# Turning SA and v as one 128-column operand, longer load rows, 320 early slots and a new order of steps in a fused attention and expert kernel

## The chip, the cores and the metric

The kernel runs on one core of one Trainium2 chip. A core has five engines with one instruction stream each: PE (TensorE: matrix products and, beside them, weight loads), DVE (VectorE), ACT (ScalarE), POOL (GpSimd) and SP (SyncE, which here issues most transfers). Each executes its own instructions in order; they wait for each other by semaphores. The metric is the device time of one launch in microseconds, the median of three runs. For the kernel before it is 639.63 us (639.16 to 650.6).

## The reference

The inputs `r, k, v, w, a, b` have 4 batches, 8 heads, 768 steps and 40 columns. Each of the 32 (batch, head) pairs runs a recurrence over a 40 x 40 state; the outputs of all heads then form 3,072 rows of 320 columns that go through a top-1 mixture of 8 experts.

```python
for t in range(S):
    y[t] = r[t] @ state
    Sa = state @ a[t]
    state = state * w[t] - outer(Sa, b[t]) + outer(v[t], k[t])
x = y, as 3072 rows of 320
logits = x @ w_gate; e = argmax(logits); g = softmax(logits)[e]
slot of a row = its rank among the rows of expert e (kept if under 768)
out = g * (relu(x @ w1[e]) @ w2[e])
```

## The kernel before

**How the recurrence is tiled.** The 768 steps are NI = 6 blocks of 128, and each block has two chunks of 64 steps (C = 64, NQ = 12 chunks in all). A pair (`pr`) is two batches with all their heads, so there are two pairs and 2 x 12 = 24 units. Within a chunk the recurrence is written as matrix products and a triangular inverse; from chunk to chunk the state is handed on. R = 104 rows hold two batches of 40 columns, at rows 0 to 39 and 64 to 103.

**The steps of a block** (`prep`, L459). `load_w`, `load_a`, `load_kb` and `load_rv` bring the inputs in. `decay` runs two scans over w on VectorE (`scan_g` L484, `scan_p` L494) and multiplies a by one of them (`mul_a` L503); `decay_k` multiplies kb by the other (`mul_kb` L506, two products, c = 0 and 1). In `load_w` each of 128 rows is cut into 8 heads of 512 bytes, because the tile `px` has one column more per head, which a memset (L489) clears.

**The steps of a unit** (`unit`, L520, and `chain`, L773). `load_v` brings v as `vu` with time on the rows; `load_x` (`load_vT`, L532) brings the same v a second time, turned on the host, as half 0 of the tile `vT`. `kk` and `nn` are products of a and kb, `iden` turns kb (L574). Then `zz` and `sa` compute SA, which `take_sa` writes into `vu` beside v. `uT` (L824) turns SA alone, as 8 transposes with 64 rows and 64 columns (L829), and `take_uT` (L838) copies the result into half 1 of `vT`. `turn` and `take_turn` turn the state. `out` is `mT` (L875: for each of 16 (k, x, r) two products with 64 x 64 weights, one on v and one on SA), `take_m`, `yy` (outputs and new state), `take_snew` and `take_y`.

**The steps between units.** For each block there is a joint inverse over both pairs (`begin2` L731, then `inverse`, `join`, `lower`, `comb`; the group `comb_b` at L713 is one of 64 products), and, behind it, the gate: `turn_y` (L958, 8 transposes of 104 columns), `logits`, and `store_x`, which writes the rows to memory for the experts. Most matrix products go through the helper `mm`, whose one line is L403. Routing (`route`, L1241) runs once for each of the six blocks: `first` (the arg-max and its running counts), `count` (three products, L1258 on), `place`, `gates`, `hot_p`, `hot_j`, `tabled`, `fold`, and for the last two blocks `index`, which makes the row lists.

**The experts** (`expert`, L1480). The rows of an expert are gathered from memory by an indirect transfer (L1384), turned, multiplied with w1 (`p` steps, L1538), clipped (`h` steps, on ACT and VectorE), multiplied with w2 (`p` steps, L1407, in chunks of 128 rows with a last one of 64 where the count asks for it), scaled and scattered to the output by an indirect transfer (`o` steps, L1413). Each expert's weights are split into a high and a low half-width part, so a hidden or output block is a sum of several products. Experts 0 and 1 are done in two parts: EA = 384 slots whose rows were routed in the first five blocks, and EB = 128 late slots. The other six take MAIN = 448 slots at once.

**What sets the order.** `ORDER` (L29) is a list written out in full, one word per step, that covers scan, gate, routing and experts. `name*n` is the next n steps of that name, `name/m` takes the m-th of its alternatives (which engines do the copy), and `name~n` puts n filler products ahead of the step: `warm` (L192) issues them as 128 x 512 products of the identity into a buffer that the step is about to overwrite. `listed` (L199) turns the list into instructions; every engine then gets its own in just that order. The `needs`, `take` and `free` of a step (see the diff) name what it waits for and which buffers it draws and gives back. All transfers of `prep` and `unit` are issued by SP, in list order.

## Time and profile before

| | |
|---|---|
| median of 3 runs | 639.63 us (639.16 to 650.6) |
| the profiled execution | 641.26 us, of which its span 639.5 us |
| mean granted clock of PE | 0.899 of full speed |
| PE, matrix products | busy 589.2 us (92% of the span), 12,503 instructions |
| PEld, weight loads | busy 445.4 us (70%), 12,503 instructions |
| DVE | busy 424.1 us (66%), 958 instructions |
| ACT | busy 271.1 us (42%), 562 instructions |
| POOL | busy 102.7 us (16%), 146 instructions |

The span runs from the first to the last instruction of one profiled execution. Busy time is the time in which an engine had an instruction in flight, so the shares of different engines overlap. A weight load runs beside the product of the instruction before it. A granted clock of 1.0 is 2.4 GHz, 0.5 is 1.2 GHz.

### The profile page before, as it was taken

To read this page: it belongs to the slowest core of one execution; us is meant where nothing else is said; L and a number is where in the kernel's file an instruction comes from. 1 tells how busy PE (TensorE), PEld (TensorE's weight loads), DVE (VectorE), ACT (ScalarE), POOL (GpSimd) and SP (SyncE) were. 2 spreads that over 40 slices of the span, in tenths; PEclk is the share of its full clock that TensorE was granted. 3 is DMA by queue.
4 is the path that set the end of the run, shared out by engine and by line. 5 is a ranking of instruction groups with operands and counts; after the bars stand their busy time and mean duration, and the time that the engine had idled before them with its cause. 6 is when DMAs were issued, how large, how long until landed. Compare 5 with 4: busy or idle time off the path is not lost.

```text
span 639.5 us, 27724 instructions
## 1 busy us (share of the span) xinstructions
PE 589.2 (92%) x12503; PEld 445.4 (70%) x12503; DVE 424.1 (66%) x958; ACT 271.1 (42%) x562; POOL 102.7 (16%) x146
## 2 busy tenths in 40 slices
PE   1869999899999989998999999899999999989995
PEld 1559788788878878877878887666665555556653
DVE  7998897779779866987388675668235371644330
ACT  9324534433255342525263354534234553545221
POOL 6100000000010010000000000221512261542212
PEclk9765997989779986998599996899989999999999
DMA  6923047404327265143303143697659777676201
GB/s 186 215 70 101 5 114 170 115 21 138 112 64 202 62 130 153 39 131 82 121 25 112 37 144 98 167 192 210 168 128 247 213 201 171 195 198 176 60 21 37
DMA packets 78948, 80.43 MB, mean 126 GB/s; under 512 B 31731, under 2 KB 67669, under 8 KB 77860
## 3 DMA queue, kind: packets, MB, share of 16 engines
q1 hardware_dynamic: 75428, 68.92, 41.0%
q0 software_dynamic: 3392, 9.64, 5.2%
q8 instruction: 100, 1.64, 1.1%
q14 instruction: 28, 0.23, 0.1%
HBM read 63.39 MB, written 10.26 MB: 115 GB/s over the span
## 4 chain that ended last, share of the span: by engine, by line
PE 61%; issue 21%; POOL 6%; DMA 1%; ACT 1%; POOLq 1%; DVE 0%; SPq 0%; another core or an unknown queue 0%; ACTq 0%
PE pp L403 24%; PE p L403 18%; PE pp L1538 3%; POOL out_dram L1413 3%; PE pp L196 3%; PE p L196 3%; POOL a L1384 2%; PE pp L574 2%; PE pp L961 2%; PE p L866 2%; PE p L1407 2%; PE pp L829 2%; PE p L1065 1%; DMA xT<-a 1%; DMA vu<-in_moe_w_dram 1%
## 5 line engine op out<-in xcount | busy, mean ns | idle before, releaser
L1413 POOL DMA_INDIRECT out_dram<-tm,ri x32 | 35.1, 1096 | 114.6 <-ACT tm L1573 90.4
L403 PE MATMUL pp<-vu,bk 128*40 128x104 f32 (+1 forms) x768 | 43.2, 272 | 0.0
L457 DVE TENSOR_TENSOR vu<-pp,mask 128x1024 f32<-128x1024 f32 x24 | 29.3, 1220 | 17.8 <-PE pp L403 13.5
L403 PEld LDWEIGHTS pp<-vu,bk 128*40 128x40 f32 x768 | 37.3, 128 | 4.6 <-issue 3.3
L453 POOL TENSOR_SCALAR_AFFINE_SELECT tm<-tm 64x512 f32<-64x512 f32 x14 | 12.4, 887 | 162.1 <-ACT tm L450 161.6
L403 PE MATMUL p<-yq,ns 64*64 64x32 f32 x768 | 31.5, 244 | 7.0 <-ACT yq L157 4.2
L403 PE MATMUL pp<-rv,vT 64*64 64x64 f32 x1536 | 34.1, 242 | 3.3 <-issue 3.1
L153 POOL COPY x<-x 128x128 f16<-128x128 f16 x18 | 8.5, 476 | 173.4 <-ACT x L153 132.8
L403 PEld LDWEIGHTS p<-yq,ns 64*64 64x64 f32 x768 | 30.0, 164 | 8.5 <-issue 7.8
L403 PEld LDWEIGHTS pp<-rv,vT 64*64 64x64 f32 x1536 | 30.2, 154 | 7.6 <-issue 6.8
L403 PE MATMUL pp<-a,kb 64*64 64x64 f32 x768 | 19.7, 251 | 16.6 <-DVE px L489 13.9
L1538 PE MATMUL pp<-xT,ns 128*128 128x448 f16 (+2 forms) x192 | 34.2, 313 | 0.0
L1384 POOL DMA_INDIRECT a<-xd,ri x25 | 28.3, 1134 | 36.3 <-DVE gs L1302 26.6
L153 ACT COPY vu<-pp 64x320 f32<-64x320 f32 x42 | 17.6, 420 | 35.6 <-PE pp L403 30.7
L582 ACT ACTIVATE bk<-pp,sgn 128x320 f32<-128x320 f32 x48 | 22.6, 526 | 20.7 <-PE pp L574 15.6
L403 PE MATMUL p<-a,kb 64*64 64x64 f32 x768 | 31.2, 236 | 0.0
L403 PEld LDWEIGHTS pp<-a,kb 64*64 64x64 f32 x768 | 16.4, 159 | 20.9 <-issue 17.6
L1538 PE MATMUL pp<-xT,px 128*128 128x448 f16 (+2 forms) x128 | 29.3, 313 | 1.9 <-DVE nt L1546 1.9
L403 PEld LDWEIGHTS p<-a,kb 64*64 64x64 f32 x768 | 28.0, 149 | 4.1 <-issue 3.7
L490 DVE TENSOR_TENSOR_SCAN gx<-px,z 104x1032 f32<-104x1032 f32 x12 | 27.7, 2308 | 3.1 <-DMA px<-in_w_dram 2.8
L510 DVE TENSOR_TENSOR kb<-kb,gx 104x1024 f32<-104x1024 f32 x24 | 29.8, 1281 | 0.0
L1546 DVE SCALAR_TENSOR_TENSOR px<-pp,rv 128x448 f16<-128x448 f32 (+1 forms) x32 | 18.6, 602 | 16.5 <-ACT rv L1543 15.0
(246 smaller groups left out, 1458.3 us busy)
## 6 DMA issues: line engine op xcount, KB each, us to landing
vu<-in_moe_w_dram SPq DMA_DIRECT2D x32, 320.0 KB
kb<-in_kb_dram SPq DMA_DIRECT2D x24, 320.0 KB
px<-in_moe_w_dram SPq DMA_DIRECT2D x13, 512.0 KB
px<-in_w_dram SPq DMA_DIRECT2D x12, 512.0 KB
vu<-in_vt_dram SPq DMA_DIRECT2D x48, 128.0 KB
vT<-in_vx_dram SPq DMA_DIRECT2D x24, 256.0 KB
xd<-x SPq DMA_DIRECT2D x24, 192.0 KB
a<-in_a_dram SPq DMA_DIRECT2D x24, 160.0 KB
```

The source lines that it names most:

```text
L153: (e.copy if e is self.nc.scalar else e.tensor_copy)(out, in_)
L196: self.nc.tensor.matmul(x, self.spare[:, 0:P], self.spare[:, None, :].to_broadcast([P, 2, 2 * P]), start=True, stop=True, skip_group_check ...
L403: TT.matmul(out, l, r, start=start, stop=True, skip_group_check=True)
L457: V.tensor_mul(out, in_, m.to_broadcast(sh))
L490: V.tensor_tensor_scan(T["gx"][0:R, 0:H * (P + 1)][:, ::-1], T["px"][0:R].rearrange("p h t -> p (h t)")[:, ::-1], z2[0:R].rearrange("p h t ...
L510: V.tensor_mul(x, x, g[:, :, None, half(c)].to_broadcast([R, H, 2, C]))
L574: TT.transpose(p[:, x, h * D:h * D + D], T["kb"][half(x, D), h, c].rearrange("p z t -> p (z t)"), ident[half(x, D), C * x:C * x + D])
L582: A.activation(U["bk"][:, x].rearrange("p h d -> p (h d)"), U["pi"][:, x, 0:HD], AF.Copy, scale=sgn[:, x:x + 1])
L1384: nc.gpsimd.indirect_dma_start(out=xt(j)[:c].rearrange("p a c -> p (a c)"), out_offset=None, in_=src[:, :], in_offset=bass.IndirectOffsetO ...
L1413: nc.gpsimd.indirect_dma_start(out=out_v[used[0] % (8 * E)][:, :], out_offset=bass.IndirectOffsetOnAxis(ap=ri.bitcast(U32)[:c, j, 1:2], ax ...
L1538: nc.tensor.matmul(s_["h", f + z][:, :n], l, rr, start=m % 7 == 0 and m < 14, stop=m >= 14)
L1546: nc.vector.scalar_tensor_tensor(s_["H"](1, f), s_["h", f][:, :n], 0.0, s_["H"](0, f), ALU.max, ALU.subtract)
```

## The change

`uT` turns v and SA together: `vu` holds SA in one half of its rows and v in the other, and each of 8 transposes now takes all 128 rows and 128 columns (1,024 columns, formerly 512). `take_uT` copies both halves into `vT` and draws that buffer itself. `mT` needs one product with 64 x 128 weights per (k, x, r), 16 instead of 32. With that `load_x`, the host-turned input `vx` and its 24 transfers go away.

`w` is packed on the host with the leading column of each head already there, so that `load_w` is 128 rows of 4,128 bytes and the memset goes; `a`, `kb` and `r` are padded from 40 to 48 rows per batch (`DL = 48`). `mul_kb` becomes two steps, c = 0 and c = 1, which may go to VectorE or GpSimd, as `mul_a` may; `nn`, `kk` and `iden` of chunk c wait for their half only. Routing runs three times: once over blocks 0 to 3, then block 4, then block 5, with a scan in place of the additions of the running counts and half-width (F16) operands in `count`. EA falls from 384 to 320; a row of experts 0 and 1 beyond the 320 early slots is placed among the late ones. The hand-over of `vT` tiles to the experts waits for `take_uT` in place of `load_x`. `ORDER` is a new list, with 2,005 steps in place of 2,029 and 116 filler products in place of 139 (after the first block 89 in place of 122).

```diff
-load_w load_kb decay0*2 decay_k0 inverse_0 load_a decay0 nn0*2 load_w load_kb decay1*2 unit decay_k1 load_v kk0
...
+load_w inverse_0 load_kb load_a decay0 load_w decay0 load_a decay_k0 load_kb decay0 decay_k0 nn0~1 load_a unit kk0
+decay1 load_v nn0 load_w decay1 nn0~3 load_v nn0 kk0/1 decay_k1 kk0~4 decay1 kk0 load_v decay_k1 nn1~2 nn1 load_a
...
-                    dma(rows(T[kind])[slice(C * z + lo * z, C * z + lo * z + D)], src[pr, i, z])
+                    dma(rows(T[kind])[slice(C * z + lo * z, C * z + lo * z + DL)], src[pr, i, z])
             return go
 
         def load_w():
             T["px"] = get("px")
-            dma(T["px"][:, :, 1:], w[pr, i].rearrange("e (h t) -> e h t", h=H))
-
-        steps("load_w")(load_w, "L0>2.7", take=["px"], gives=("load_w", n))
-        steps("load_a")(loads("a", a, lambda x: x.rearrange("p h t -> p (h t)")), "L0>.86&L0>.86", take=["a"],
+            dma(T["px"].rearrange("p h t -> p (h t)"), w[pr, i])
+
+        steps("load_w")(load_w, "L0>1.8", take=["px"], gives=("load_w", n))
...
-            V.memset(T["px"][:, :, 0:1], 0.0)
...
-            V.tensor_mul(T["a"][0:R], T["a"][0:R], T["px"][0:R, :, 0:P])
-
-        def mul_kb():
+            engine().tensor_mul(T["a"][0:R], T["a"][0:R], T["px"][0:R, :, 0:P])
+
+        def mul_kb(c):
             g = T["gx"][0:R, 1:].rearrange("p (h t) -> p h t", t=P + 1)[:, :, 1:]
-            for c in range(2):
-                x = T["kb"][0:R, :, c]
-                V.tensor_mul(x, x, g[:, :, None, half(c)].to_broadcast([R, H, 2, C]))
-            put("gx", T["gx"])
+            x = T["kb"][0:R, :, c]
+            engine().tensor_mul(x, x, g[:, :, None, half(c)].to_broadcast([R, H, 2, C]))
+            if c:
+                put("gx", T["gx"])
 
         add = steps(f"decay{pr}")
-        add(scan_g, "V2.4", take=["gx"] + ["g0"] * (i > 0), needs=[("load_w", n)])
+        add(scan_g, "V2.4", take=["gx"] + ["g0"] * (i > 0), needs=[("load_w", n)], gives=("gx", n))
         add(scan_p, "V2.6", gives=("px", n))
-        add(mul_a, "V1.22", needs=[("load_a", n)], gives=("a", n))
-        steps(f"decay_k{pr}")(mul_kb, "V2.3", needs=[("px", n), ("load_kb", n)], free=["gx"], gives=("kb", n))
+        add(mul_a, "V1.22|G2.35", needs=[("load_a", n)], gives=("a", n))
+        add = steps(f"decay_k{pr}")
+        for c in range(2):
+            add(lambda c=c: mul_kb(c), "V1.15|G2.35", needs=[("px" if c else "gx", n), ("load_kb", n)], free=["gx"] * c, gives=("kb", n, c))
...
-        def load_vT():
-            U["vT"] = get("vT")
-            dma(U["vT"][:, 0].rearrange("p u t -> p (u t)"), vx[pr, q])
-
-        steps("load_v")(load_v, "L0>.5&L0>.5", take=["vu"], gives=("load_v", n))
-        PLAN[0] += HC / 2
-        steps("load_x")(load_vT, "L0>.86", take=["vT"], gives=("load_x", n))
-        PLAN[0] -= HC / 2
+        steps("load_v")(load_v, "L0>.65&L0>.65", take=["vu"], gives=("load_v", n))
...
-        add(nn, "P.64", needs=[("a", nT), ("kb", nT)], take=["pp"])
+        add(nn, "P.64", needs=[("a", nT), ("kb", nT, c)], take=["pp"])
...
-                    y = half(1 - x)
-                    TT.transpose(p[:, x, k * C:k * C + C], U["vu"][y, x, k, C:3 * C], ident[y, y])
+                    TT.transpose(p[:, x, k * P:k * P + P], U["vu"][:, x, k, C:3 * C], ident)
...
-            copy(U["vT"][:, 1].rearrange("p (x k) t -> p x (k t)", x=2), U["pt"][:, :, 0:4 * C])
+            U["vT"] = get("vT")
+            copy(flat(U["vT"]), U["pt"].rearrange("p x t -> p (x t)"))
...
-                        for z in range(2):
-                            mm(p[half(z), r, u * C:u * C + C], U["vT"][half(r), int(z != x), u, :], T["rv"][half(r), c, u, :],
-                               True)
+                        mm(p[:, r, u * C:u * C + C], U["vT"][half(r), u, :], T["rv"][half(r), c, u, :], True)
...
-        more(uT, "P.6", needs=[("vu", n)], take=["pp"])
-        more(take_uT, "A.56|V.62", needs=[("load_x", n)], free=["pp"], gives=("uT", n))
+        more(uT, "P.9", needs=[("vu", n)], take=["pp"])
+        more(take_uT, "A1.04|V1.2", take=["vT"], free=["pp"], gives=("uT", n))
...
+    sets = [tuple(range(NI - 2)), (NI - 2,), (NI - 1,)] if NI > 2 else [(i,) for i in range(NI)]
+    for m, G_ in enumerate(sets):
+        PLAN[0] = G_[-1] * GT + 1.5 * GT
+        add = steps(f"rout{late(G_[-1])}")
...
-            acc = s_["acc"] = glob.tile([P, B + 1, E], F32, name="acc")
-            nc.gpsimd.memset(acc[:, 0, :], 0.0)
-            for m in range(B):
-                nc.vector.tensor_add(acc[:, m + 1, :], acc[:, m, :], oh[:, m, :])
+            s_["oh"] = oh_.rearrange("p e t -> p t e")[:, 1:n + 1]
+            s_["ne"] = best(glob, lg[:, tiles, :], n, NM, s_["oh"])
+            x, y, z = (x.rearrange("p e t -> p (e t)") for x in (acc_, keep_on, oh_))
+            nc.vector.tensor_tensor_scan(x, y, z, 0.0, ALU.mult, ALU.add)
 
         def count():
 
             ps = s_["ps"]
-            oh, acc = (x.rearrange("p t e -> p (t e)") for x in (s_["oh"], s_["acc"]))
-            nc.tensor.matmul(ps[:, 0:B * E], up, oh, start=True, stop=False)
-            nc.tensor.matmul(ps[:, 0:B * E], ones, acc[:, 0:B * E], start=False, stop=True)
-            nc.tensor.matmul(ps[:, B * E:(B + 1) * E], ones, acc[:, B * E:], start=True, stop=True)
+            acc = acc_.rearrange("p e t -> p t e")
+            nc.tensor.matmul(ps[:, 0:n * E], up, s_["oh"], start=True, stop=False)
+            nc.tensor.matmul(ps[:, 0:n * E], ones, acc[:, 0:n], start=False, stop=True)
+            nc.tensor.matmul(ps[:, n * E:(n + 1) * E], ones, acc[:, n], start=True, stop=True)
...
+            if EARLY and G_[-1] == NI - 2:
+                over = glob.tile([P, B, 2], F32, name="over")[:, 0:n]
+                for e in range(2):
+                    nc.vector.tensor_scalar(over[:, :, e], rank[:, :, e], float(e * CS + EA), float(CS - EB - EA), ALU.is_ge,
+                                            ALU.mult)
+                nc.vector.tensor_add(rank[:, :, 0:2], rank[:, :, 0:2], over)
...
-    out["w"] = np.concatenate([x, x[:, :, :, 0:C - D]], 3).reshape(B // 2, NI, P, H * P)
-    out["a"] = rows(inputs["a"])
+    x = np.concatenate([x, x[:, :, :, 0:C - D]], 3).reshape(B // 2, NI, P, H, P)
+    out["w"] = np.pad(x, [(0, 0)] * 4 + [(1, 0)]).reshape(B // 2, NI, P, H * (P + 1))
+
+    def padded(x, back=0):
+        y = np.zeros(x.shape[:3] + (48,) + x.shape[4:], x.dtype)
+        for z in range(2):
+            lo = (48 - D) * z * back
+            y[:, :, z, lo:lo + D] = x[:, :, z]
+        return y
+
+    out["a"] = padded(rows(inputs["a"]))
     kb = np.stack([rows(inputs[x]).reshape(B // 2, NI, 2, D, H, 2, C) for x in "kb"], 6)
     kb[:, :, 1] = kb[:, :, 1, :, :, :, ::-1]
-    out["kb"] = kb.reshape(B // 2, NI, 2, D, 2 * H * P)
-    out["rv"] = cols(inputs["r"])
+    out["kb"] = padded(kb.reshape(B // 2, NI, 2, D, 2 * H * P))
+    out["rv"] = padded(cols(inputs["r"]), 1)
...
-    out["vx"] = v.transpose(0, 1, 5, 6, 2, 4, 3).reshape(B // 2, S // C, P, H * C)
```

## Rows read from the trace of the kernel before

**Rows 1.** Page, DMA queues: queue and kind, packets, MB, share of 16 engines.

```profile
q8 instruction: 100, 1.64, 1.1%
```

**Rows 2.** Windows, scan stage: length, busy PE, PEld, DVE, ACT, POOL, clock, DMA, GB/s.

```profile
73.20:422.00 348.80, 332.93 (x9891) 280.24 (x9883) 265.49 (x664) 143.58 (x333) 19.36 (x33) 0.88 0.39 105
```

**Rows 3.** Timeline of PE: start, us, line, operation, tiles, count, idle before and releaser.

```profile
122.67 0.56 PE L403 MATMUL p<-nt,qq 64*32 64x32 f32 x22
125.92 1.28 PE L403 MATMUL p<-nt,qq 64*32 64x32 f32 x41 [2.69 <-issue]
...
234.09 0.79 PE L403 MATMUL p<-yq,ns 64*64 64x32 f32 x13 [1.95 <-issue]
```

**Rows 4.** Windows, four of the seven stretches at the granted clock 0.50.

```profile
104.60:111.40 6.80, 6.80 (x134) 5.94 (x133) 3.69 (x3) 3.04 (x7) 0.09 (x1) 0.50 0.48 140
125.10:131.90 6.80, 5.98 (x118) 4.59 (x117) 1.54 (x3) 2.50 (x5) 0.00 (x0) 0.50 0.26 74
234.30:251.40 17.10, 17.10 (x319) 13.71 (x315) 6.93 (x11) 5.20 (x12) 0.00 (x0) 0.50 0.38 102
411.80:418.60 6.80, 6.46 (x142) 5.74 (x144) 4.51 (x7) 2.54 (x6) 0.00 (x1) 0.50 1.14 184
```

**Rows 5.** DMA queues in the window 123.4 to 125 us, the instruction queue.

```profile
q8 instruction: 1, 0.02, 3.6%
```

**Rows 6.** Timeline of SP's queue, two issues of `load_x`.

```profile
122.70 0.61 SPq L168 DMA_DIRECT2D vT<-in_vx_dram  x1
...
227.91 0.35 SPq L168 DMA_DIRECT2D vT<-in_vx_dram  x1
```

**Rows 7.** Timeline of PE, groups whose lengths serve as prices.

```profile
197.43 0.93 PE L961 MATMUL pp<-ident,px 104*128 104x104 f32 x8
198.19 0.38 PE L196 MATMUL p<-ident 128*128 128x512 f16 x1
198.41 0.30 PE L1258 MATMUL p<-oh,upper 128*128 128x32 f32 x2
...
201.41 0.69 PE L574 MATMUL pp<-ident,kb 40*128 40x40 f32 x16
201.93 0.44 PE L829 MATMUL pp<-ident,vu 64*128 64x64 f32 x8
202.31 0.39 PE L196 MATMUL p<-ident 128*128 128x512 f16 x1
...
399.72 1.14 PE L403 MATMUL pp<-rv,vT 64*64 64x64 f32 x64
400.68 0.63 PE L403 MATMUL pp<-vu,tm 64*64 64x40 f32 x32
```

**Rows 8.** Timeline of the start, VectorE and PE.

```profile
5.21 2.31 DVE L490 TENSOR_TENSOR_SCAN gx<-px,z 104x1032 f32<-104x1032 f32 x1 [2.77 <-DMA px<-in_w_dram]
...
10.30 2.35 DVE L510 TENSOR_TENSOR kb<-kb,gx 104x1024 f32<-104x1024 f32 x2
...
13.88 1.15 PE L403 MATMUL pp<-a,kb 64*64 64x64 f32 x29 [13.88 <-DVE px L489]
```

**Rows 9.** Timeline of PE in the experts, products with w1 and w2.

```profile
435.96 1.14 PE L1538 MATMUL pp<-xT,ns 128*128 128x384 f16 x6
436.93 0.33 PE L1538 MATMUL pp<-xT,kb 128*128 128x384 f16 x1
...
620.16 0.31 PE L1407 MATMUL p<-kb,nt 128*128 128x320 f16 x1
...
623.52 0.33 PE L1407 MATMUL p<-kb,nt 128*64 128x320 f16 x2
...
625.27 0.31 PE L1407 MATMUL p<-kb,nt 128*128 128x320 f16 x1
```

**Rows 10.** Timeline of POOL and PE, the late rows of experts 0 and 1.

```profile
446.34 1.04 POOL L1384 DMA_INDIRECT vT<-xd,ri  x1 [10.73 <-DVE ri L1301]
...
457.29 0.28 PE L1538 MATMUL pp<-xT,px 128*128 128x128 f16 x2
```

More of the change, by code (lines that the diff above doesn't have):

```diff
@@ L940, in chain @@
         more = steps(f"out{pr}")
-        more(mT, "P1.5", needs=[("uT", n), ("load_rv", (pr, i))], take=["pp"], free=["vT"])
+        more(mT, "P1.6", needs=[("uT", n), ("load_rv", (pr, i))], take=["pp"], free=["vT"])
         more(take_m, "A1.0 G2.4|V1.22", free=["pp"])
@@ L1041, in scan_part @@
             gate(Ts[pr, i])
-        PLAN[0] = i * GT + 1.5 * GT
-        add = steps(f"rout{late(i)}")
+    sets = [tuple(range(NI - 2)), (NI - 2,), (NI - 1,)] if NI > 2 else [(i,) for i in range(NI)]
+    for m, G_ in enumerate(sets):
+        PLAN[0] = G_[-1] * GT + 1.5 * GT
+        add = steps(f"rout{late(G_[-1])}")
         L_ = {}
-        first, count, place, gates, hot_p, hot_j, fold, index = route(i, L_)
-        add(first, "V1.9", needs=[("logits", (pr, i)) for pr in range(2)] + [("gated", i - 1)] * (i > 0),
-            gives=("one_hot", i))
@@ L1048, in scan_part @@
-        add(lambda f=count, L=L_: (L.update(ps=get("p1")), f()), "P1", take=["p1"], gives=("counted", i))
-        add(lambda f=place, L=L_: (f(), put("p1", L["ps"])), "V.75", needs=[("placed", i - 1)] * (i > 0), free=["p1"],
-            gives=("placed", i))
-        add(gates, "A.12 V.5", gives=("gated", i))
-        def take_hot(f=hot_p, L=L_):
-            L["hp"] = get("tm")
-            f(L["hp"])
-        def take_hot_j(f=hot_j, L=L_):
-            L["hj"] = get("yq")
-            f(L["hj"])
@@ L1061, in tabled @@
-        def tabled(L=L_):
-            p = L["pt"] = get("p1")
-            hp, hj = (L[x].rearrange("p x y -> p (x y)") for x in ("hp", "hj"))
-            for bi in range(B):
-                TT.matmul(p[:, 0:NV], hp[:, bi * P:bi * P + P], hj[:, bi * NV:bi * NV + NV], start=bi == 0, stop=bi == B - 1)
-            put("tm", L["hp"])
-            put("yq", L["hj"])
-        add(take_hot, "V.12 V.12 V.6", take=["tm"])
-        add(take_hot_j, "V.27 V.27 V.27", take=["yq"])
-        add(tabled, "P1.2", take=["p1"], free=["tm", "yq"])
@@ L1072, in scan_part @@
-        add(lambda f=fold, L=L_: (f(L["pt"]), put("p1", L["pt"])), "V.17", needs=[("tab", i - 1) if i else ("fill", 0)], free=["p1"],
-            gives=("tab", i))
+        first, count, place, gates, hot_p, hot_j, fold, index = route(m, G_, L_)
+        n = len(G_)
+        add(first, f"V{1.1 + .2 * n:.2f}", needs=[("logits", (pr, i)) for pr in range(2) for i in G_] + [("gated", m - 1)] * (m > 0),
+            gives=("one_hot", m))
+        add(lambda f=count, L=L_: (L.update(ps=get("p1")), f()), "P.5", take=["p1"], gives=("counted", m))
@@ L1103, in scan_part @@
     PLAN[0] = last * GT
-    ends = [("kb", (pr, last)) for pr in range(2)]
+    ends = [("kb", (pr, last), 1) for pr in range(2)]
     hand("gx", "gx", 1, ["W"], ends)
@@ L1121, in scan_part @@
     for y in ("xt", "hh", "hh"):
-        hand("vT", "vT", 1, [y], [("load_x", (pr, NQ - 1)) for pr in range(2)])
+        hand("vT", "vT", 1, [y], [("uT", (pr, NQ - 1)) for pr in range(2)])
     for y in (["sv", "sv"], ["W", "W"], ["W", "W"], ["sv", "W"]):
@@ L1137, in tile_kernel @@
     NF = F // P
-    EA, EB = 384, P
-    EARLY = cap > EA and CS >= EA + EB and S // P > 2
+    EA, EB = 320, P
+    EARLY = cap >= EA + EB and S // P > 2
     SX = 64.0
@@ L1614, in tile_kernel @@
     at = T0 + TAIL_AT
-    r0, r1 = ([("fill", 0), ("table", NI - z)] + [("store_x", (pr, i)) for pr in range(2) for i in range(NI - z + 1)]
+    r0, r1 = ([("fill", 0), ("table", LAST + 1 - z)] + [("store_x", (pr, i)) for pr in range(2) for i in range(NI - z + 1)]
               for z in (2, 1))
```

367 lines of the change are left out of this document (201 added, 166 removed).

## Prediction

> **What bounds the kernel now.** I read the page first: PE is the busiest engine, 589.2 of a span of 639.5 us (the table above). Then the stages. From 73.2 us, where the second block's inverse begins, to 422 us, where the scan's last product has gone and the experts start, PE is busy 332.9 of 348.8 us and VectorE 265.5 [rows 2]. So PE's in-order stream sets the end there; from 422 us on it does so too.
>
> Next I asked what that stream loses. PE is idle for 348.8 - 332.9 = 15.9 us of the stage. The long gaps are not waits for data: at 122.67 a `comb_b` group of 64 products stops after 22, stays away for 2.69 us with nothing named but "issue", and goes on [rows 3]. Products in the middle of one group need nothing new, so the engine had no instructions. The queue view shows why: the page has 100 "instruction" packets with 1.64 MB, thus 16 KB each [rows 1], which at 1.64 MB over about 25,000 PE instructions (products and weight loads) is one packet for some 250 of them. Just such a packet lands between 123.4 and 125.0, inside the gap [rows 5]. It came late because the data queue was full. The other gaps have the same form: eight of 0.6 to 2.8 us, at 102, 123, 168, 232, 279, 297, 385 and 405 us, and some short ones near 410 (the two that the sum uses are shown).
>
> Each costs more than its length. After them PE runs at the granted clock 0.50 (1.2 of 2.4 GHz) though it is busy nearly throughout. There are seven such stretches in the stage, of 6.8, 6.8, 13.6, 17.1, 20.4, 10.2 and 6.8 us [rows 4], 81.7 us together, in which half the speed, 40.9 us, is lost. With the 15.9 idle that is 57 us of 348.8 that no arithmetic asks for, some 7 us for each of eight gaps.
>
> **The change part by part.**
>
> *Start.* VectorE's first scan waits for w until 5.21 us, two kb products then take 2.35 us, and PE's first product follows a at 13.88 [rows 8]. The new list puts one kb half behind `mul_a`, and `nn` for c = 0 no longer needs it: 2.35/2 = 1.2 us earlier. w lands as 128 rows of 4,128 bytes instead of 1,024 pieces of 512; its wait was 2.77 us. Bounds are 0 and 2.8; I take 0.5, since the copy's size is unchanged and its fixed part stays. The memset of px's first column (70 ns) goes too. Sum **-1.7 us** (-1.2 to -4); VectorE is the chain of this stage, so it carries through.
>
> *Turning SA and v as one.* There are 24 units (2 pairs, 12 chunks). `uT` has 8 transposes of 64 columns, 201.93 to 202.31 = 0.38 us. The new ones have 128 rows and 128 columns. The nearest row is `turn_y`, 8 transposes of 104: 197.43 to 198.19 = 0.76 us; by columns 0.76 x 128/104 = 0.94, thus +0.56 a unit (bounds 0.76 flat, +0.38; 1.3, +0.9) [rows 7]. Sum **+13.4 us** (+9 to +22).
>
> `mT` goes from 32 products (64 instructions, 399.72 to 400.68 = 0.96 us) to 16 (32 instructions) with 64 x 128 weights. The same weight shape stands in `iden`, 16 instructions in 201.41 to 201.93 = 0.52, 32 ns each, and in `uT`, 8 in 0.38, 48 ns each [rows 7]. So 1.04 or 1.52 us. I take 1.04, the longer run, in which the start counts least: +0.08 a unit, **+2 us**; the other end is +13.
>
> The Trainium skill ("TensorE: Matmul & The Clock Gate", LDWEIGHTS) speaks against it: a weight load takes columns/1.2 ns whatever the rows, so 107 ns for 128 columns. By that, as an estimate, `mT` would take 32 x 107/2 = 1.7 us with two tiles loading side by side, +18 us in all; 32 ns for each 40 x 128 load in [rows 7] does not agree with it, and the sum goes by the row.
>
> `take_uT` copies 1,024 columns instead of 512, on ScalarE, which is busy 143.6 of 348.8 us [rows 2]: nothing on the path, since the other pair's products lie under it; without that cover it would be one more copy of the old size (about 0.6 us) per unit, 14 us. It now takes its vT buffer there and not at a load; three buffers stand against one use at a time, so nothing queues behind it.
>
> *Fillers and routing on PE.* Between 73 us and the first expert the list's fillers fall from 122 to 89. One costs 0.22 us (198.19 to 198.41) [rows 7]: **-7.3 us**. Routing runs three times instead of six with half-width operands; a `count` has three pairs like the one at 198.41 (0.30 us, its end overlapping the next), so three fewer give 2 to 2.7: **-2.5 us**.
>
> *VectorE.* Three routing sets fewer, four products moved to POOL, the memsets and more `take_nn` on ScalarE take work off VectorE. Of the four, no POOL row shows a price; each can hold up an `nn` by what it takes beyond VectorE's 1.2 us, and POOL is busy 19.4 us of the stage [rows 2]. I count nothing for all of this: it had 83 us to spare in the stage [rows 2] and no long gap of PE waits for it. If it were the bound, the gain would be at most that work, some 14 us.
>
> *DMA and the gaps.* The 24 `load_x` copies of 256 KB go (6.3 MB); a, kb and r grow by 48/40 (+3.1 MB). SP's queue loses 24 issues. PE has 24 x 64 = 1,536 instructions fewer of 19,774 in the stage, so six packets of code fewer. Two gaps have a `load_x` just ahead: it was issued at 122.70 and at 227.91, 0.5 us before the gap at 123.2 and 4.2 us before that at 232.1 [rows 6]. They cost 2.69 + 6.8/2 = 6.1 and 1.95 + 17.1/2 = 10.5 us [rows 3, 4]. I take these two as gone and the others as staying: **-17 us**. The bounds are 0 (the gaps only move) and half of the 57, -28.
>
> *Early slots.* Experts 0 and 1 do 320 rows first instead of 384. A product of 384 columns takes 0.97/6 = 0.162 us (435.96 to 436.93); 64 columns fewer are 0.027, and 2 x 64 products give 3.4 us. The last chunk of each turns from 128 wide (620.16 to 623.52, 3.4 us) to 64 wide (623.52 to 625.27, 1.75): 3.2 us more [rows 9]. This stretch is PE's without a break, but the last routing must be ready behind it: its first gather starts at 446.34 and the products on it at 457.29 [rows 10]. Gather and transpose need some 6 us of those 11, so about 5 us of the 6.6 are free; I take **-4 us** (-1 to -6.6).
>
> Sum: -1.7 + 13.4 + 2 - 7.3 - 2.5 - 17 - 4 = -17.1 us. The profiled run took 641.26 us around its span of 639.5, beside a median of 639.63; I put the difference on the median: **622 us**.
>
> **The rivals.**
>
> *The gaps only move.* The code packets still meet full queues elsewhere in the new order. For it: gaps also stand at 297 and 385 with no `load_x` ahead. Against it: fewer bytes and fewer instructions. Without the 17 us the sum is -0.1: 639.5 us.
>
> *More gaps go.* Half of the 57 us instead of 17: 639.6 - 0.1 - 28 = 611 us. For it: the old w copy lay in the same queue before the gap at 123.
>
> *Longer rows hold up the code.* At the data engines w's 4-KB rows and a, kb and r on more engines may stand in front of each code packet. Place: the packets fetched while a block's loads land. For it: the full queue at 123.4 [rows 5]. Price: 7 us for each gap that is new; the point from which it decides is one gap more than now, 639.5 + 7 = 646, and with three it is 660 us, slower. Against it: the bytes fall on balance. The Trainium skill ("DMA: Bandwidth & Descriptors", Queues, rings and completion order) has the rule for this: an engine drains a whole packet of one queue before it turns to the next. No row here shows one packet waiting for another.
>
> *Wide weight loads.* `mT` at `uT`'s pace of 48 ns: 622 + 13.4 - 2 = 633 us. By the Trainium skill's rule on weight loads it is an estimate of 622 + 16 = 638; [rows 7] do not bear it out.
>
> **How the numbers follow.** The forecast (622) has 0.36, more gaps gone (611) 0.17, gaps moved (639.5) 0.22, wide loads (633) 0.12, longer rows (646 to 660) 0.13. 2% is 12.8 us, about what a measurement of this kernel can tell from no change, so faster means under 626.8. More gaps gone lies there, and most of the forecast, whose own range is 614 to 630 by the bounds of start, `uT` and tail: 0.17 + 0.33 = **0.50 faster**. Gaps moved, wide loads, the rest of the forecast and the milder end of longer rows are within: **0.40**. The harder end, over 652.4, has **0.10**. The range of 606 to 646 leaves out that end and the few cases in which more than half of the gaps go.
>
> **What would show it.** `uT` groups of 0.9 us and `mT` groups of 1.0; a scan stage with fewer than seven stretches at 0.50 and no 2-us "issue" gap in the middle of a group; PE's first product near 12.2; experts' first stretch some 6 us shorter. It is wrong if the stage's idle plus half-clock loss stays at 57 us or more, if `mT` takes 1.5, or if PE waits for the last routing before the late rows of experts 0 and 1.

## The result and the profile after

| | before | after |
|---|---|---|
| median | 641.15 us (4 runs, 639.16 to 650.6) | 629.69 us (4 runs, 629.11 to 630.6) |
| ratio | | 0.985 (95% interval 0.980 to 0.989) |
| span of the profiled execution | 639.5 us | 628.8 us |
| mean granted clock | 0.899 | 0.948 |
| to the second block's inverse | 73.2 us | 75.1 us |
| from there to the first expert product (the scan stage) | 348.9 us | 343.7 us |
| from there to the end | 217.4 us | 210.0 us |

The changed kernel is 1.5% faster, inside the range of 606 to 646 us and 8 us above the forecast of 622. Single executions of one kernel scatter by up to 4%, so a ratio with an interval counts only those near the kernel's fastest (within 1.5%), and the profiles of three kernels below (*after, old loads*, *after, w in pieces* and *before, turned, narrow*) are of slower ones, whose loss is too high rather than too low. The three stretches give +1.9, -5.2 and -7.4 us, together the -10.7 us between the spans.

The page of the changed kernel, three lines: engines, then two DMA queues with packets, MB and share of 16 engines.

```profile
PE 575.8 (92%) x11685; PEld 446.4 (71%) x11685; DVE 416.6 (66%) x877; ACT 282.8 (45%) x564; POOL 111.0 (18%) x154
...
q1 hardware_dynamic: 61460, 65.62, 42.1%
...
q8 instruction: 93, 1.52, 1.0%
```

PE has 818 products and 818 weight loads fewer and fetches 93 packets of code in place of 100 [rows 1]. The windows view of the changed kernel, first the scan stage, then its four stretches at the granted clock 0.50 (columns as in [rows 2]):

```profile
75.10:418.80 343.70, 330.87 (x9029) 288.60 (x9028) 261.32 (x596) 157.13 (x334) 25.42 (x31) 0.96 0.38 97
...
160.30:167.10 6.80, 6.80 (x96) 6.07 (x96) 4.09 (x5) 1.16 (x3) 0.00 (x0) 0.50 0.01 4
252.50:255.90 3.40, 3.22 (x41) 3.10 (x41) 0.69 (x1) 1.36 (x5) 0.00 (x0) 0.50 0.18 64
300.30:310.50 10.20, 8.12 (x114) 7.38 (x115) 4.91 (x8) 2.15 (x5) 2.62 (x2) 0.50 0.01 3
409.50:419.70 10.20, 9.79 (x119) 8.31 (x118) 3.85 (x5) 3.02 (x6) 1.72 (x4) 0.50 0.72 118
```

These rows split the stage into two parts, and the rest of this document works with them. The **loss** is PE's idle time plus half of the time at 0.50. Before it was 15.9 + 81.7/2 = 56.8 us [rows 2, 4]; now it is 343.7 - 330.9 = 12.8 us idle and 29.8/2 = 14.9 (the last stretch cut at the stage's end), 27.7 us. The **work** is what is left: 292.0 us before, 316.0 now. So the loss fell by 29 us, which the prediction put at 17, and the work rose by 24 us, which it put at 5.6. Two errors went opposite ways, and the total looked better than its steps: that it came so near was in part luck.

The timeline of PE of the changed kernel (columns as in [rows 3]), `uT` (L827) and `mT` (L408, 64*128), and then the longest gap that is left:

```profile
199.08 1.09 PE L827 MATMUL pp<-ident,vu 128*128 128x128 f32 x8
200.11 2.00 PE L408 MATMUL pp<-rv,vT 64*128 64x64 f32 x32
202.04 1.15 PE L408 MATMUL p<-a,kb 64*64 64x64 f32 x32
...
297.51 0.43 PE L408 MATMUL pp<-D,a 64*64 64x40 f32 x10
302.38 0.87 PE L408 MATMUL pp<-D,a 64*64 64x40 f32 x20 [4.43 <-issue]
```

`uT` takes 1.03 us from start to start (forecast 0.94), but `mT` takes 202.04 - 200.11 = 1.93 us for 32 instructions, where 64 took 0.96 [rows 7] and 1.04 was forecast. Gaps in the middle of a group still exist, at places with no `load_x` near, since there is none. Not all of the idle time is of this kind: PE waited for nothing that is named in 15.1 of its 15.9 idle us before, and in 9.7 of 12.8 now.

The start of the changed kernel, VectorE and PE:

```profile
4.38 2.31 DVE L494 TENSOR_TENSOR_SCAN gx<-px,z 104x1032 f32<-104x1032 f32 x1 [1.95 <-DMA px<-in_w_dram]
...
10.58 1.23 DVE L513 TENSOR_TENSOR kb<-kb,gx 104x1024 f32<-104x1024 f32 x1 [1.02 <-DMA kb<-in_kb_dram]
...
12.35 1.22 DVE L508 TENSOR_TENSOR a<-a,px 104x1024 f32<-104x1024 f32 x1 [0.55 <-DMA a<-in_a_dram]
...
13.63 1.19 PE L408 MATMUL pp<-a,kb 64*64 64x64 f32 x30 [4.19 <-DVE a L508]
```

w lands 0.83 us earlier than in [rows 8], but now VectorE waits 1.02 us for kb and 0.55 us for a, and PE's first product comes 0.25 us earlier, not 1.7. The stretch up to the second block's inverse even grew by 1.9 us. The first inverse's run of small steps on VectorE starts at 27.75 us (27.85 before), but the product of PE behind it comes 0.96 us later than before, and about as much again is lost from there on. The two lines of PE's timeline, before and after:

```profile
42.42 3.62 PE L403 MATMUL p<-yq,ns 64*64 64x32 f32 x64 [4.17 <-ACT yq L157]
```

```profile
43.38 3.62 PE L408 MATMUL p<-yq,ns 64*64 64x32 f32 x64 [9.71 <-ACT yq L161]
```

### The profile page after: what moved, and what is told of

It reads as the page before. It is cut to its first block, busy times and chain, and to the rows that moved or that the text cites. A ratio compares the mean times of both kernels' runs of the same rounds, so it can differ in the third digit from the quotient of the medians.

```text
span 628.8 us, 25977 instructions
## 1 busy us (share of the span) xinstructions
PE 575.8 (92%) x11685; PEld 446.4 (71%) x11685; DVE 416.6 (66%) x877; ACT 282.8 (45%) x564; POOL 111.0 (18%) x154
## 4 chain that ended last, share of the span: by engine, by line
PE 69%; issue 14%; DMA 4%; DVE 4%; POOL 3%; ACT 3%; another core or an unknown queue 0%; POOLq 0%; SPq 0%; DVEq 0%; ACTq 0%
PE pp L408 25%; PE p L408 17%; PE pp L1555 8%; PE p L1424 6%; PE pp L827 3%; PE pp L200 3%; POOL out_dram L1430 2%; PE pp L573 2%; PE p L865 2%; PE pp L958 2%; DMA kb<-in_kb_dram 2%; PE p L200 2%; DMA a<-xd,ri 1%; DMA nt<-in_moe_w_dram 1%; DVE tmp L632 1%
## 5 line engine op out<-in xcount | busy, mean ns | idle before, releaser
L408 PE MATMUL pp<-rv,vT 64*128 64x64 f32 x768 | 50.2, 281 | 0.9 <-issue 0.4
L408 PEld LDWEIGHTS pp<-rv,vT 64*128 64x128 f32 x768 | 46.8, 194 | 4.5 <-ACT vT L157 1.7
L408 PE MATMUL pp<-vu,bk 128*40 128x104 f32 (+1 forms) x768 | 41.0, 263 | 1.4 <-issue 1.4
L408 PEld LDWEIGHTS pp<-vu,bk 128*40 128x40 f32 x768 | 35.6, 124 | 5.6 <-issue 4.3
L408 PE MATMUL p<-yq,ns 64*64 64x32 f32 x768 | 29.0, 235 | 11.4 <-ACT yq L161 10.8
L408 PEld LDWEIGHTS p<-yq,ns 64*64 64x64 f32 x768 | 27.6, 153 | 12.9 <-ACT yq L161 11.4
L1560 ACT ACTIVATE nt<-pp 128x448 f16<-128x448 f32 (+2 forms) x48 | 18.6, 437 | 39.9 <-PE pp L1555 30.4
L157 ACT COPY vT<-pp 128x1024 f32<-128x1024 f32 x24 | 24.2, 1013 | 26.8 <-PE pp L827 23.7
L581 ACT ACTIVATE bk<-pp,sgn 128x320 f32<-128x320 f32 x48 | 22.5, 526 | 23.9 <-PE pp L573 13.2
L1424 PEld LDWEIGHTS <-nt 128*128 128x128 f16 (+1 forms) x272 | 22.4, 100 | 14.1 <-issue 3.5
L200 PE MATMUL pp<-ident 128*128 128x512 f16 x72 | 24.3, 400 | 8.9 <-ACT pp L426 8.9
L494 DVE TENSOR_TENSOR_SCAN gx<-px,z 104x1032 f32<-104x1032 f32 x12 | 27.7, 2308 | 6.2 <-ACT ns L161 3.3
L1590 ACT ACTIVATE tm<-p,gs 128x320 f32<-128x320 f32 x24 | 12.7, 528 | 41.7 <-PE p L1424 24.5
L161 ACT ACTIVATE ns<-pp 32x256 f32<-32x256 f32 (+1 forms) x54 | 24.3, 450 | 14.8 <-PE pp L408 13.8
L1555 PE MATMUL pp<-xT,xu 128*128 128x448 f16 (+2 forms) x128 | 28.8, 307 | 2.1 <-DMA xT<-a 1.3
L632 DVE TENSOR_TENSOR tmp<-xu,nu 128x48 f32<-128x48 f32 (+11 forms) x138 | 28.7, 224 | 2.3
```

The lines of the kernel that those rows point to most:

```text
L157: (e.copy if e is self.nc.scalar else e.tensor_copy)(out, in_)
L161: (e.mul if e is self.nc.scalar else e.tensor_scalar_mul)(out, in_, x)
L200: self.nc.tensor.matmul(x, self.spare[:, 0:P], self.spare[:, None, :].to_broadcast([P, 2, 2 * P]), start=True, stop=True, skip_group_check ...
L408: TT.matmul(out, l, r, start=start, stop=True, skip_group_check=True)
L494: V.tensor_tensor_scan(T["gx"][0:R, 0:H * (P + 1)][:, ::-1], T["px"][0:R].rearrange("p h t -> p (h t)")[:, ::-1], z2[0:R].rearrange("p h t ...
L632: V.tensor_mul(tv(), diag(s_["xu"])[:, :, t0:t1, s:s + 1].to_broadcast([P, nb, n, m]), diag(s_["nu"])[:, :, s:s + 1, 0:m].to_broadcast([P, ...
```

## The experiments

Each kernel ran with the kernel before beside it on the same chip. Times differ between chips and between rounds on one chip (the medians of the kernel before were 643 to 650 us in these runs), so ratios are compared, and the stage's loss and work from the profiles. Each profile is a single execution; the two of the changed kernel differ by 8.8 us in the loss and by 1 us in the work. The kernel before was profiled only in the first round. Where no interval stands, the ratio is that of the medians of all executions. Instructions are products and weight loads in the stage.

| kernel | median, us | ratio to before (95%) | stage | idle | at 0.50 | loss | work | instructions |
|---|---|---|---|---|---|---|---|---|
| before | 641.15 | 1 | 348.9 | 15.9 | 81.7 | 56.8 | 292.0 | 19,766 |
| after | 629.69 | 0.985 (0.980-0.989) | 343.7 | 12.8 | 29.8 | 27.7 | 316.0 | 18,053 |
| after, repeated | 641.73 | 0.993 (0.987-0.998) | 351.4 | 12.6 | 47.8 | 36.5 | 315.0 | 18,053 |
| after, narrow `mT` | 647.12 | 1.016 (1.004-1.028) | 359.1 | 32.3 | 61.4 | 63.0 | 296.1 | 19,589 |
| after, narrow `mT` and `uT` | 658.70 | 1.036 (1.023-1.049) | 368.5 | 36.5 | 92.2 | 82.6 | 285.9 | 19,972 |
| after, with `load_x` copies | 641.55 | 1.003 (0.995-1.012) | 348.2 | 13.4 | 34.1 | 30.4 | 317.8 | 18,053 |
| after, 384 early slots | 641.46 | 0.987 (medians) | 342.6 | 14.4 | 20.5 | 24.7 | 317.9 | 18,053 |
| after, no fillers | 656.62 | 1.022 (1.013-1.031) | 370.1 | 32.4 | 94.4 | 79.6 | 290.5 | 17,867 |
| after, old loads | 623.80 | 0.967 (0.956-0.978) | 335.2 | 7.2 | 23.9 | 19.2 | 316.0 | 18,053 |
| after, 40 rows | 618.91 | **0.963 (0.959-0.968)** | 329.2 | 5.6 | 13.7 | 12.4 | 316.7 | 18,053 |
| after, w in pieces | 639.23 | 0.988 (0.981-0.995) | 348.7 | 13.9 | 36.5 | 32.2 | 316.6 | 18,053 |
| before, turned as one | 658.22 | 1.018 (medians) | 361.4 | 15.4 | 30.7 | 30.7 | 330.7 | 18,230 |
| before, turned, narrow | 666.96 | 1.032 (medians) | 375.6 | 24.8 | 102.4 | 76.0 | 299.6 | 20,150 |
| before, long rows | 666.64 | 1.027 (1.012-1.043) | 366.8 | 29.8 | 92.6 | 76.1 | 290.7 | 19,766 |

### Is the slow `mT` a cost?

```diff
-                        mm(p[:, r, u * C:u * C + C], U["vT"][half(r), u, :], T["rv"][half(r), c, u, :], True)
+                        for z in range(2):
+                            mm(p[half(z), r, u * C:u * C + C], U["vT"][half(r), u, half(z)], T["rv"][half(r), c, u, :], True)
```

> The changed kernel with one edit: mT as 32 products with 64 x 64 weights again, on the same vT tile, in place of 16 with 64 x 128. Theory (wide weights cost): in the changed kernel a pair of 64 x 128 products takes 112 ns, where four of 64 x 64 took 58 ns before, so mT is 1.83 us a unit and not the 1.04 of the prediction; undone, mT is 0.96 to 1.1 us, 24 x 0.85 = 20 us less on PE's path, 608 to 611 us. Rival (the slow mT was cover): PE's stream gets 768 products and as many weight loads more, so code packets come due more often, gaps and half-clock stretches come back, and the time falls by 0 to 8 us only, 622 to 630 us.

Windows of its scan stage, and its PE timeline at one of its gaps:

```profile
78.60:437.70 359.10, 326.83 (x9799) 280.94 (x9796) 262.02 (x598) 157.04 (x335) 24.99 (x31) 0.91 0.38 92
```

```profile
172.13 1.16 PE L408 MATMUL pp<-rv,vT 64*64 64x64 f32 x64
173.12 0.72 PE L408 MATMUL p<-yq,ns 64*64 64x32 f32 x19
176.05 2.23 PE L408 MATMUL p<-yq,ns 64*64 64x32 f32 x42 [2.22 <-issue]
```

The work fell by nearly what the first theory said (20 us), 315.0 to 296.1 us, and `mT` took 173.12 - 172.13 = 0.99 us. The kernel became **slower** all the same: the loss rose from 36.5 to 63.0 us. The gap above stands 19 products behind a narrow `mT`, in a group that had begun; a packet of code landed in it. The narrow group is 128 instructions (64 products, 64 loads) in 0.99 us, 129 per us; the wide one is 64 in 1.93 us, 33 per us. So the theory of wide weights was right on the price and wrong on the time, and the rival, that the slow `mT` is time in which code arrives, was stronger than it expected of itself.

The packet records show that most such gaps are waits for code. In the scan stages of the 14 profiles PE stands still for more than 0.3 us 218 times, and in 169 of these it goes on between 1 and 2 us after a code packet has landed; of moments picked at random only one in five lies so.

The next run went further in the same direction, with `uT` narrow too (16 transposes of 64 rows, row half z into bank z):

```diff
-                    TT.transpose(p[:, x, k * P:k * P + P], U["vu"][:, x, k, C:3 * C], ident)
+                    for z in range(2):
+                        TT.transpose(p[:, z, (x * 4 + k) * C:(x * 4 + k) * C + C], U["vu"][half(z), x, k, C:3 * C], ident[half(z), half(z)])
...
-            copy(flat(U["vT"]), U["pt"].rearrange("p x t -> p (x t)"))
+            copy(U["vT"].rearrange("p u (z t) -> p z u t", z=2), U["pt"].rearrange("p z (u t) -> p z u t", t=C))
...
```

> The changed kernel with mT as 32 products with 64 x 64 weights, and uT as 16 transposes of 64 rows and 64 columns (row half z into bank z) in place of 8 of 128 rows and 128 columns; take_uT copies the same 1,024 columns. Theory (PE's stream sets the end): a 128 x 128 transpose takes 109 ns, a pair of the 64-row ones took 62 ns before, so uT goes from 0.88 to about 0.5 us and mT from 1.83 to 1.0: 24 x (0.85 + 0.38) = 29 us less, about 600 us. Rival (uT waits for take_sa and lies beside other work): the uT part gives nothing and the time is that of the kernel with the mT edit alone; or gaps come back with the added instructions, 615 to 630 us.

```profile
78.00:446.50 368.50, 332.01 (x9989) 285.69 (x9990) 261.17 (x597) 157.10 (x334) 24.36 (x30) 0.87 0.38 90
```

Another 10.2 us of work went, and 19.6 us of loss came. In these two runs, less arithmetic in more instructions is slower.

### Did `load_x` hold up the code?

The copy is issued for each unit as soon as a `vT` tile is free:

```diff
...
+                Y["vT"] = get("vT")
+                nc.sync.dma_start(Y["vT"][:, 0:4, :].rearrange("p u t -> p (u t)"), vt[Y["T"]["pr"], Y["q"]].rearrange("x p y -> (x p) y"))
...
```

> The changed kernel with the 24 copies of 256 KB back: each unit's v is also loaded a second time, 128 rows of 2,048 bytes, into the vT tile before take_uT overwrites it (the copied values are not used). Theory (those copies held up PE's code): in the scan stage the half-clock stretches grow from 30.6 us to 50 or more and code packets come late at more places, +8 to +17 us, 638 to 647 us. Rival (the new order and the other loads made the gaps go): stretches stay near 30 us, and the time within 3 us of 630.

```profile
79.30:427.50 348.20, 334.83 (x9028) 292.00 (x9027) 260.72 (x596) 156.56 (x334) 24.86 (x30) 0.95 0.42 110
```

The stage moves 110 GB/s in place of 94 in the repeated kernel, and its loss is 30.4 us beside 36.5. The copies bring no gaps back. The ratio is 1% above that of the repeated kernel, with intervals that overlap; the medians of the two on this chip are 641.55 and 641.73 us, so the difference lies in the kernel before beside them. In the new order, then, the step that gave `load_x` two gaps and 17 us falls; in the old order the copies were taken out only together with `uT` and `mT` (below).

### The early slots

```diff
...
-    EA, EB = 320, P
+    EA, EB = 384, P
```

> The changed kernel with 384 early slots in place of 320 (the third chunk of experts 0 and 1 whole, and its place in the list exchanged with the second, as the program orders whole chunks). Theory (PE's stream sets the experts' end): 128 products are 0.027 us longer and two chunks 1.6 us longer, 6.6 us, so 636 us, with the stretch from the first expert to PE's end going from 202.2 to about 208.8 us. Rival (PE waits for the late rows anyway): the longer early work fills a wait, and the time rises by 0 to 3 us.

Its window from the first expert product to PE's end:

```profile
414.60:627.20 212.60, 206.09 (x1447) 122.78 (x1447) 93.18 (x173) 86.18 (x162) 68.53 (x60) 0.98 0.62 156
```

The stretch is 212.6 us, where the changed kernel has 202.4 in its first profile and 204.9 in the repeated one; freed of idle time and of half the 6.8 us at 0.50, the work is 202.7 us beside 197.1. That is 5.6 us of the 6.6 foreseen, and no wait for the late rows takes them back. The median of the whole kernel says nothing here, since other stages moved too.

### The parts alone, in the kernel before

The changed kernel unedited as a measure, and three runs that put one part of the change into the kernel before, with its old list (without the `load_x` steps where those are gone).

> The changed kernel without an edit, as the measure for the other runs beside it on the same chip. All theories: 0.98 to 0.99 of the kernel before, and in its scan stage about 316 us of work at full clock (length less PE's idle time less half of the half-clock stretches), 13 us idle and 30 us at half clock, as in its first profile.

> The kernel before with one part of the change alone: v and SA turned as one (uT as 8 transposes of 128 columns, mT as 16 products with 64 x 128 weights, take_uT takes the vT buffer and copies all of it, no load_x), with the old loads, the old routing, 384 early slots and the old list less its load_x steps. Supply theory (PE is held up by the arrival of its instructions: the narrow mT alone made the changed kernel slower, 359 us for its scan stage in place of 344, though its work fell from 316 to 296 us): the stage has 1,536 instructions fewer, its work rises from 292 to about 323 us, and idle time and half-clock loss fall from 57 us by 25 or more: 630 to 645 us. Rival (PE's arithmetic sets the end, and the two gaps beside load_x go): 640 + 31 - 17 = 654 us or more.

> The same as the run of v and SA turned as one in the kernel before, but with narrow operands: mT as 32 products with 64 x 64 weights, uT as 16 transposes of 64 rows. Supply theory: some 20,150 instructions in the stage, more than before, so in spite of 25 to 30 us less work it is not faster than the wide form and may be slower, 635 to 660 us, with idle time and half-clock loss of 57 us or more. Rival (arithmetic, and load_x held up the code): 640 + 5 - 17 = 628 us, 25 us or more faster than the wide form.

> The kernel before with the load part of the change alone: w as 128 rows of 4,128 bytes with its leading columns (and no memset of them), a, kb and r as 48 rows for each batch; load_x stays. Supply theory: the number of PE's instructions is unchanged, so the time stays within 5 us of the kernel before and the half-clock stretches of the stage stay at 65 to 95 us. Rival (the small pieces of w held up the code packets): the stretches fall from 82 to 55 us or less and the time by 10 us or more.

The edits of the two kinds of load in the last, the loads alone (the padding on the host and the memset are those of the change):

```diff
...
-                    dma(rows(T[kind])[slice(C * z + lo * z, C * z + lo * z + D)], src[pr, i, z])
+                    dma(rows(T[kind])[slice(C * z + lo * z, C * z + lo * z + DL)], src[pr, i, z])
...
-            dma(T["px"][:, :, 1:], w[pr, i].rearrange("e (h t) -> e h t", h=H))
+            dma(T["px"].rearrange("p h t -> p (h t)"), w[pr, i])
...
```

Windows of the four scan stages, in the order of the expectations, one fence each:

```profile
77.60:429.00 351.40, 338.82 (x9028) 295.52 (x9026) 262.94 (x596) 156.79 (x334) 24.92 (x30) 0.93 0.38 94
```

```profile
73.80:435.20 361.40, 346.05 (x9131) 297.26 (x9123) 267.60 (x665) 155.15 (x335) 22.50 (x36) 0.96 0.33 87
```

```profile
74.00:449.60 375.60, 350.79 (x10090) 295.48 (x10081) 267.56 (x665) 155.23 (x335) 22.31 (x36) 0.86 0.32 85
```

```profile
79.40:446.20 366.80, 336.96 (x9892) 283.36 (x9884) 267.06 (x658) 144.97 (x335) 21.52 (x36) 0.87 0.45 108
```

Turned as one, in the old list: the loss fell by 26 us, as the supply theory said, to 30.7; but the work rose by 38.7 us, more than the 31 expected, and the time, 648.7 to 672.4 us, came out nearer the rival's 654 than the 630 to 645 of the supply theory. By itself, in the old order, this part loses: the two executions that count took 648.7 and 653.5 us, the six of the kernel before 637.3 to 645.1, a loss of some 1.4%. The narrow form has 31 us less work and is not faster: its one execution that counts took 652.0 us, like the wide form's, where the rival asked for 25 us less. So less work in more instructions bought no time in this order of steps either; that it is slower than the wide form is not shown, and its loss of 76 us comes from the slowest of its four executions. The long rows missed both expectations: nothing or a gain was expected, and they cost 2.7%, with the loss 19 us above that of the kernel before (profiled in another round). That opened the next question.

### Which rows?

Both loads undone in the changed kernel (still no `load_x`), and then each by itself. The edit of a, kb and r:

```diff
-                    dma(rows(T[kind])[slice(C * z + lo * z, C * z + lo * z + DL)], src[pr, i, z])
+                    o = lo + DL - D if lo else 0
+                    dma(rows(T[kind])[slice(C * z + o * z, C * z + o * z + D)], src[pr, i, z, (o - lo) * z:(o - lo) * z + D])
```

> The changed kernel with the load part undone: w as 1,024 pieces of 512 bytes again (and the memset of the leading columns), a, kb and r as 40 rows for each batch; no load_x. Theory (long rows hold up PE's code, as the load part alone did in the kernel before, where it raised the stage from 349 to 367 us): idle time and half-clock loss of the scan stage fall below the 36.5 us of the unedited changed kernel on such a chip, and the ratio to the kernel before from 0.993 to 0.97 or 0.98. Rival (what counts is where the list puts the loads among PE's dense groups, not their rows): the ratio stays within 0.985 to 1.0, with PE's first product 0.5 us or more later.

> The changed kernel with a, kb and r loaded as 40 rows for each batch in place of 48; w stays 128 rows of 4,128 bytes. Theory (the rows of a, kb and r hold up the code: 3.1 MB more, on more engines at once): most of the gain of the old loads shows here, idle time and half-clock loss of the scan stage near 19 us and a ratio of 0.965 to 0.975 to the kernel before. Rival (w's 4,128-byte rows do): 0.985 to 0.995, as the changed kernel unedited.

> The changed kernel with w as 1,024 pieces of 512 bytes again and the memset of the leading columns; a, kb and r stay 48 rows. Theory (w's 4,128-byte rows hold up the code): ratio 0.965 to 0.975 to the kernel before, with VectorE's first scan some 1 us later. Rival (the 48 rows do): 0.985 to 0.995.

Windows of the scan stages of the three, in that order; the second kernel also at the load of the last two kb tiles:

```profile
75.60:410.80 335.20, 327.99 (x9029) 286.44 (x9028) 261.24 (x604) 156.56 (x334) 25.53 (x30) 0.96 0.33 92
```

```profile
74.10:403.30 329.20, 323.60 (x9029) 282.53 (x9027) 260.63 (x596) 156.74 (x335) 26.66 (x31) 0.98 0.32 94
...
282.00:288.50 6.50, 6.50 (x191) 6.19 (x188) 5.93 (x6) 4.49 (x9) 0.00 (x0) 1.00 0.54 204
```

```profile
79.50:428.20 348.70, 334.76 (x9029) 291.17 (x9028) 262.67 (x603) 156.99 (x334) 25.65 (x31) 0.95 0.39 95
```

The rows of a, kb and r are it: with 40 rows the loss is 12.4 us and the ratio 0.963, the fastest kernel here (the changed kernel had 0.985 and 0.993, and the intervals do not meet); with w cut up again and 48 rows kept it is 0.988, as unedited. The work is the same 316 to 317 us in all three.

The changed kernel at the load of its last two kb tiles, windows view:

```profile
291.00:299.40 8.40, 6.94 (x212) 6.56 (x210) 6.55 (x7) 4.93 (x10) 0.00 (x0) 1.00 1.00 171
```

With 48 rows all 16 DMA engines are busy here (share 1.00) and 171 GB/s move; with 40 rows the share is 0.54 and 204 GB/s move. At three earlier loads of kb the shares differ likewise (0.80 to 1.09 with 48 rows, 0.53 to 0.71 with 40), the rates hardly (175 to 210 GB/s beside 179 to 221). The packet records of the traces agree with the shares: in the scan stage packets of 8,192 bytes (kb's rows) are most often 16 in flight at once with 48 rows and take 649 ns on average, and 10 in flight with 40 rows, 423 ns. The Trainium skill ("DMA: Bandwidth & Descriptors", Why a DMA increments its semaphore by 16 and not by 1) has the rule: a DMA uses the largest number of engines up to 16 that divides its rows, 10 for 40 and 16 for 48; the trace agrees. What it means for PE is seen at the same group of products that stood 4.43 us in the changed kernel; with 40 rows its timeline reads:

```profile
288.93 0.43 PE L408 MATMUL pp<-D,a 64*64 64x40 f32 x10
289.55 0.55 PE L408 MATMUL pp<-D,a 64*64 64x40 f32 x20 [0.18 <-issue]
```

The code packet that the group needs is not late there: one moved from 287.02 to 288.01 us, while kb's rows moved. In the changed kernel none moved between 291.74 and 299.36 us, and the one that started then landed at 300.94, 1.44 us before the group went on. How 48 rows hold up code is open. That with 40 rows a packet goes by one of the six engines left alone is possible, but the records don't name engines. Over all of kb's loads in the stage, code packets start equally seldom in both kernels (0.14 to 0.15 per us, 0.21 to 0.22 over the whole stage), but with 48 rows these loads fill 40 us in place of 35, and a code packet within one takes 1.45 us on average in place of 1.01 (6 packets and 5).

Half of the 12.4 us still lost with 40 rows has another cause. Near the scan's end PE's `logits` wait 3.13 us for `take_y` on VectorE, and 6.8 us at 0.50 follow, 6.5 us of loss:

```profile
394.99 0.74 PE L408 MATMUL p<-px,wge 128*16 128x128 f32 x16 [3.13 <-DVE px L920]
```

The changed kernel has the same wait (2.33 us at 406.8); the kernel before has none of this size there.

### The fillers

The changed kernel without the 93 filler products behind the start of its second block (each `name~n` there written as `name`).

> The changed kernel without the 93 filler products behind the start of its second block (the 23 ahead of it stay). Arithmetic theory (PE's stream sets the end, and a filler costs its 0.22 us): the work of the stage falls from 316 to about 297 us and the time by some 17 to 20 us, a ratio of 0.965 to the kernel before. Supply theory (fillers give 0.22 us for two instructions, time in which code arrives): PE's instructions come no faster, idle time and half-clock loss rise by most of what the work falls, and the ratio stays between 0.985 and 1.01.

Its scan stage, and one gap in its PE timeline:

```profile
77.20:447.30 370.10, 337.65 (x8936) 306.89 (x8935) 262.30 (x596) 156.75 (x334) 25.12 (x31) 0.87 0.36 90
```

```profile
318.44 0.98 PE L408 MATMUL p<-yq,ns 64*64 64x32 f32 x26
323.56 1.71 PE L408 MATMUL p<-yq,ns 64*64 64x32 f32 x29 [4.15 <-issue]
```

The work fell by 24.5 us, and the loss rose by 43 us. A filler is two instructions in 24.5/93 = 0.26 us. Taken away, the dense groups stand closer together, and PE runs out of code in their middle, here 26 products into a group of 64. The supply theory had the sign and still expected too little.

## Why the prediction came out as it did

The prediction gave 0.50 to a gain of 2% or more; the 1.5% that came lies in the 0.40 for less than 2% either way. One of its own signs of being wrong appeared, `mT` over 1.5 us. Two more of its signs of being right stayed away: there is a 4.43-us "issue" gap in the middle of a group, and PE's first product comes at 13.63 us, not near 12.2. The rest came out as foreseen.

**What bounds the kernel.** The prediction saw late code packets and the half clock behind each, and put a price on them, but then added up PE's arithmetic as if the loss were a thing apart. The runs show that the two hang together. PE works at 57 instructions per us of work in the changed kernel (18,053 in 316) and at 66 to 70 in the kernel before and in its narrow forms (19,766 in 292; 19,972 in 286), and the loss goes with that pace: 25 to 37 us at 55 to 57 and 57 to 83 us at 66 to 70, less only where the changed kernel has its 40 rows back (12 and 19 at 57). The kernel without fillers, 62 per us and a loss of 80, stands out from the row: its average is lower, but its dense groups follow each other more closely, which is the likely reason and was not tried apart. In the three edits of the changed kernel that took PE time away but hardly an instruction (narrow `mT`, narrow `uT`, no fillers), waiting gave back more than was taken: 26.5 us for 18.9, 19.6 for 10.2, 43 for 24.5.

**`mT`, the term that was mis-sized.** +2 us was taken from `iden`'s 32 ns an instruction; 1.93 us a unit was measured for 0.96 in [rows 7], or 1.09 by the median over the units of before: +0.84 to +0.97, 20 to 23 us in all. The start times show a pair of 64 x 128 products every 112 ns, where four of 64 x 64 took 58 ns. `iden` was the wrong row: it is a transpose, and the pairs of that shape start every 62 ns. The nearest price was the one that the prediction put aside: the Trainium skill ("TensorE: Matmul & The Clock Gate", LDWEIGHTS) lets a load take its columns over 1.2 ns, 107 ns for 128 columns and 53 for 64, and an estimate by it was 1.7 us for `mT`; the 112 and 58 ns agree with it.

**`uT`, the early slots, routing.** Mechanism and size were right: 1.03 us for 0.94 forecast, and 5.6 to 6.4 us for a tail that the sum put at 4 (work from the first expert on: 203.5 us before, 197.1 after). PE waited for no late row; a wait of 1.31 us for early rows, at 430.3 us, is new.

**The gaps.** The sum had -17 us for two gaps beside `load_x`. The loss fell by 29 us, but not for that reason: with the copies back it stayed at 30. Most of it fell because the wide `mT` has 1,536 instructions fewer and takes longer over them; undone, 26 us of loss return, and put into the old list, the wide operands take away 26 us. The rival *more gaps go* named the right size (-28) with the wrong cause.

**Longer rows hold up the code.** This rival had 0.13 and was the one with a mechanism that the runs bear out, in part: the 48 rows cost the changed kernel 2 to 3%, w's 4,128-byte rows nothing. It was judged by bytes ("the bytes fall on balance"), and bytes were not the measure: 5 MB of `load_x` in the stage cost no loss, 2 MB of padding rows cost 15 to 24 us of it (27.7 and 36.5 beside 12.4). How many engines are taken at once, and for how long by one packet, would fit both, but this is argued and not shown; with `load_x`'s 2,048-byte rows and kb's 8,192 the two are not separated here.

**The fillers.** -7.3 us was booked as a gain. As work it was right; in time it was hardly one, since 93 fillers fewer cost some 19 us by the ratios (1.022 and 0.993). What the change's own 33 fewer cost was not tried alone.

**The start.** 1.2 + 0.5 us were foreseen, 0.25 came. VectorE was the chain, but the next thing late behind w was kb and then a, which the prediction did not name, and the first inverse then ended later than before. So the stretch cost 1.9 us where 1.7 were to be gained.

So the total of 629.7 is 622 with +18 for more work (nearly all `mT`), -12 for more of the loss gone, +3.6 for the start and -3.4 for the tail, which makes 628.2, and 1.5 for the scatter of both medians. Wide operands alone (some +1.4%) and long rows alone (+2.7%) lose in the old list, so the rest of the change must, if the parts add up, gain more than the 1.5% of the whole. Some 6 us of that are the early slots; how much is due to the list's order, how much to the routing sets, stays open.

## What to carry to other kernels

Where an in-order engine stops in the middle of a group with no releaser named, count its instructions, not its arithmetic: fewer and larger ones can be worth more than faster ones, and filler work between dense groups can pay for itself. Look for the DMA share at such places; here a transfer on all 16 engines with long packets hurt more than one on 10, and padding rows from 40 to 48 changed just that. And when a total comes out right, check its terms against the trace before believing the reasons.
